# Eight dK stores as GpSimd scatters behind the next Q scaling, in place of five dV stores

## The chip, the cores and the metric

The kernel runs on one core of a Trainium2 chip. A core has five engines with queues of their own: TensorE (PE in the profile; its weight loads are PEld), VectorE (DVE), ScalarE (ACT), GpSimd (POOL) and SyncE (SP). Sixteen DMA engines move data between HBM and the on-chip memory SBUF; matmuls write to PSUM. A transfer that SyncE issues is given to the DMA engines in hardware (queue q1 in the profile); for one that GpSimd issues, software on GpSimd writes what each DMA engine is to do (queue q0). Fetches of program code go over the same 16 engines (q8, q14).

The metric is the time of one execution on the device in microseconds: 669.41 us is the median of 3 runs of the kernel before (668.9 to 669.71). Beside these there is one execution under the profiler, from which all durations below come.

## The reference, cut to what matters

The kernel computes grouped-query attention and its gradients: the output o, and dq, dk and dv for a given `grad_out`.

```python
B, Hq, Hkv, Sq, Sk, D = 32, 32, 4, 4, 2048, 128      # all bfloat16

def _fwd_reference(q, k, v):
    k = jnp.repeat(k, Hq // Hkv, axis=1)
    v = jnp.repeat(v, Hq // Hkv, axis=1)
    scores = jnp.einsum("bhqd,bhkd->bhqk", q, k) * D ** -0.5
    p = _softmax(scores, axis=-1)
    return jnp.einsum("bhqk,bhkd->bhqd", p, v)

def reference(q, k, v, grad_out):
    out, vjp = jax.vjp(_fwd_reference, q, k, v)
    return (out, *vjp(grad_out))
```

K and V are read once and dK and dV written once: 32 batches x 4 heads x 2048 x 128 of two bytes are 67 MB for each of the four, and with q, grad_out, o and dq some 272 MB in all.

## The kernel before, in words

The batch is the outer loop, and one batch is one stage of about 20 us. In HBM, K, V, dK and dV stand as two tensors each (half 0 and half 1, two heads per half), with 128 rows per batch: a row has 4096 bfloat16 (`ROW`, 8192 bytes). Half 0 and half 1 of K carry 128 columns more, q and grad_out (`LONG`, 8448 bytes); half 1 of dV and of dK carry o and dq there. So a batch has four loads (LK and LV, halves 0 and 1) and four stores (SV and SK, halves 0 and 1), each of 128 rows, about 1 MB.

All of them go through 20 row tiles in SBUF (`slots`, `row` in the profile). A slot is filled by a load, read, overwritten by results or the next load, and stored.

The stages of a batch, by the names in the kernel: transposes of q and grad_out (QT), of K and V (KT, VT) on PE and their copies out of PSUM (KTe, VTe and so on, on ACT or DVE); scores (S), row minimum (MX), exponential (EX), reciprocal (RC); on GpSimd the scaling of grad_out by the reciprocal (dop, line 290), a small product (rs, line 302) and the scaling of q (qp, line 293); the transposes of the probabilities (ET) and the output (O, Oe); dP (DP) and dS (DS); their transposes (DT) and dQ (DQ, DQe); dV and dK (DV, DK, line 334) and their evictions to row tiles (DVe, DKe, line 340).

The order of everything is written out by hand: the string `PLAN` has four characters for each unit (name, part, engine or place, buffer), the loop at its end emits them one after another, and each engine runs its own in that order. The units of neighbouring batches are interleaved: the qp of a batch stands behind the last DKe, the DQe and the SK of half 1 of the batch before.

SyncE issues every load and nearly every store in the order of the plan. Each of its DMAs updates one of eight semaphores in turn and waits until the DMA that had it last has landed, so that at most eight are in flight.

Five stores are not SyncE's. For the batches in `SPREAD` (4, 6, 8, 10, 12) the store of half 0 of dV is made by GpSimd right behind the qp of the following batch, as indirect DMAs (scatters) that take the row numbers from a small tile `at` that holds 0, 1, 2, ... Each of the five is made of two pieces, rows 126 and 127 and then rows 0 to 125, that go to output tensors of their own; the host only puts them back in their places. Two more scatters, of 3 and of 13 words, stand before the first and behind the last of them (`turns`); they store nothing that is used.

Of the kernel before, what the change touches and what calls it, by code (L numbers as in the profile page):

```python
# [10 lines left out]
BF16 = mybir.dt.bfloat16  # L11
# [3 lines left out]
P = 128  # L15
NH = 4
ROW = 2 * 16 * P
LONG = ROW + P
# [3 lines left out]

SPREAD = (4, 6, 8, 10, 12)
PIECES = ((126, 2), (0, 126))

# [143 lines left out]
def kernel(  # L169
# [10 lines left out]
    spread,  # L180
    turns,
):
    nc = tc.nc
# [7 lines left out]
    const_pool, sm_pool = pool("const", 1), pool("small", 4)  # L191
# [6 lines left out]
    at = const_pool.tile([P, 1], mybir.dt.int32, name="at")  # L198
    nc.gpsimd.iota(at[:], pattern=[[0, 1]], base=0, channel_multiplier=1)

    def scatter(out, in_):
        nc.gpsimd.indirect_dma_start(out=out, in_=in_, in_offset=None,
                                     out_offset=bass.IndirectOffsetOnAxis(ap=at[0:in_.shape[0], 0:1], axis=0))

    scatter(turns[0], at[0:3, 0:1])
    junk = const_pool.tile([P, D], BF16, name="junk")
# [26 lines left out]
    def emit(u):  # L233
        b, name, i = u.b, u.name, u.part
        t = T[b]
# [14 lines left out]
        elif name == "QTe":  # L250
            t["qdt"] = sm_pool.tile([P, 2 * P], BF16, name="qdt_sb", bufs=3)
            copy16(u.where, t["qdt"][:], t["qtp"])
# [38 lines left out]
        elif name == "qp":  # L291
            t["qp"] = sm_pool.tile([P, D], BF16, name="qp_sb", bufs=2)
            nc.gpsimd.tensor_scalar(out=t["qp"][:], in0=t["q"], scalar1=t["rinv"][:], scalar2=scale, op0=ALU.mult,
                                    op1=ALU.mult)
            if b - 1 in SPREAD:
                for (first, count), piece in zip(PIECES, spread[SPREAD.index(b - 1)]):
                    scatter(piece, T[b - 1]["DV", "out", 0][first:first + count, 0:ROW])
                if b - 1 == SPREAD[-1]:
                    scatter(turns[1], at[0:13, 0:1])
        elif name == "rs":  # L300
# [24 lines left out]
        elif name == "DS":  # L325
            w = slice(2 * QW * i, 2 * QW * i + 2 * QW)
            nc.vector.scalar_tensor_tensor(out=t["ds"][:, w], in0=t["DP", i], scalar=t["dl"][:], in1=t["e"][:, w],  # L327
                                           op0=ALU.subtract, op1=ALU.mult)
        elif name in ("DV", "DK"):
            i, g = divmod(i, 2)  # L330
            acc = t[name, i, g] = bank(u, 2)
            moving, still = ("e", "dop") if name == "DV" else ("ds", "qp")
            for h in (2 * g, 2 * g + 1):
                nc.tensor.matmul(acc[:, QW * (h % 2):QW * (h % 2) + QW], lhsT=t[still][rows[h], :],  # L334
                                 rhs=t[moving][rows[h], QW * i:QW * i + QW], start=True, stop=True,
                                 tile_position=(32 * h, 0))
        elif name in ("DVe", "DKe"):
            i, g = divmod(i, 2)
            copy = nc.scalar.copy if u.where == "A" else nc.vector.tensor_copy
            copy(out=heads_of(t[name[:2], "out", g])[:, :, QW * i:QW * i + QW],  # L340
                 in_=t[name[:2], i, g].rearrange("p (h c) -> p h c", h=2))
        elif name == "SK" and i in LAST:
            g, first, runs, n = LAST[i]
            part = lambda row: (row[:, 0:ROW].rearrange("p (h c) -> p h c", h=2)[:, :, first:first + n] if runs == 2
                                else row[:, first:first + n])
            nc.sync.dma_start(out=part(dk_r[g][b]), in_=part(t["DK", "out", g]))
        elif name in ("SV", "SK"):
            n = LONG if i else ROW
            if not (name == "SV" and i == 0 and b in SPREAD):
                nc.sync.dma_start(out=(dv_r if name == "SV" else dk_r)[i][b], in_=t["D" + name[1], "out", i][:, 0:n])  # L350
# [48 lines left out]
```

## Time and profile before

| | before |
|---|---|
| median of 3 runs | 669.41 us |
| profiled execution, its own time | 671.37 us |
| its span, first to last instruction | 669.2 us |
| granted TensorE clock, mean | 0.984 |
| PE / DVE / ACT / POOL busy | 91% / 86% / 85% / 8% |
| bytes moved by DMA, mean rate | 273.96 MB, 409 GB/s |
| SyncE's queue q1: packets, MB, share of the 16 engines | 37536, 267.40, 96.3% |
| GpSimd's queue q0: packets, MB, share | 1024, 5.24, 2.0% |
| code fetches q8 and q14: packets, MB | 68 and 24, 1.11 and 0.20 |
| scatters on GpSimd | 12, of about 1 us each |

How to read it: the busy time of an engine is a share of the whole span. The slices divide the span into 40 equal parts, and each digit is a busy share in tenths. The DMA row is the mean over the 16 engines. The queues have the packets that were moved: one packet is one row of a transfer, or a 4-byte word that tells of a landing. The chain is the work that ended last, followed back to what released it; a piece of it that is a DMA reaches from its issue to its landing. In the tables of waits the columns are the waiting engine and line, what it waited for, the total in us, how often, and the longest.

### The profile page before, as it was taken

How to read it: one execution, taken by the hardware profiler on the slowest of the kernel's cores; microseconds unless marked ns; L12 is line 12 of the kernel's file. 1: busy time of each engine (PE TensorE's matmuls, PEld its weight loads, DVE VectorE, ACT ScalarE, POOL GpSimd, SP SyncE). 2: the span in 40 equal slices, each digit the busy share in tenths (PEclk: the TensorE clock that was granted, in tenths of full speed). 3: DMA queues.
4: the chain of work that ended last, by engine and by line, in shares of the span. 5: the costliest groups of instructions: out<-in, count | busy, mean ns of one | idle time of the engine just before them, and what ended most of it. 6: DMA issues, size and time to landing. Idle time of an engine off the chain costs nothing.

```text
span 669.2 us, 20668 instructions
## 1 busy us (share of the span) xinstructions
PE 608.9 (91%) x8768; PEld 399.7 (60%) x8768; DVE 572.6 (86%) x736; ACT 569.7 (85%) x802; POOL 50.8 (8%) x115
## 2 busy tenths in 40 slices
PE   5998999999998999899999999998989999898991
PEld 5665666566665666566666666655656556565650
DVE  1988899898998989799899999978989879888991
ACT  4997899898988889799899999978888879878992
POOL 1000000101010010200000000000000000000000
PEclk9999999999999999999999999989999989989996
DMA  9999999999999999999999999999999999999966
GB/s 347 420 423 423 425 411 424 415 419 423 412 423 415 425 416 416 423 407 422 421 424 422 425 425 423 424 423 423 419 408 415 420 421 420 410 417 422 404 276 247
DMA packets 38652, 273.96 MB, mean 409 GB/s; under 512 B 4512, under 2 KB 4512, under 8 KB 6560
## 3 DMA queue, kind: packets, MB, share of 16 engines
q1 hardware_dynamic: 37536, 267.40, 96.3%
q0 software_dynamic: 1024, 5.24, 2.0%
q8 instruction: 68, 1.11, 0.6%
q14 instruction: 24, 0.20, 0.1%
HBM read 136.31 MB, written 136.31 MB: 407 GB/s over the span
## 4 chain that ended last, share of the span: by engine, by line
PE 63%; DMA 17%; ACT 7%; DVE 7%; issue 4%; SPq 0%; DVEq 0%; ACTq 0%
PE psum L260 33%; DMA out_dram<-row 16%; PE psum L334 13%; PE psum L312 9%; PE psum L274 8%; ACT row L340 5%; DVE vt_sb L228 4%; DMA row<-in_k_dram 1%; DVE row L340 1%; DVE ds_sb L327 1%; ACT e_sb L283 1%; PE psum L249 0%; DVE row L320 0%; DVE e_sb L279 0%; ACT vt_sb L226 0%
## 5 line engine op out<-in xcount | busy, mean ns | idle before, releaser
L340 ACT CAST row<-psum 128x1024 bf16<-128x1024 f32 x292 | 291.5, 1021 | 47.6 <-PE psum L334 43.9
L260 PE MATMUL psum<-ident,row 128*128 128x128 f32 x2048 | 287.3, 282 | 12.9 <-DMA row<-in_k_dram 6.8
L340 DVE CAST row<-psum 128x1024 bf16<-128x1024 f32 x220 | 265.0, 1218 | 16.2 <-PE psum L334 7.6
L260 PEld LDWEIGHTS psum<-ident,row 128*128 128x128 f32 x2048 | 223.6, 143 | 78.0 <-issue 24.8
L226 ACT COPY kt_sb<-psum 128x512 f32<-128x512 f32 x190 | 110.3, 600 | 10.4 <-PE psum L260 10.3
L226 ACT COPY vt_sb<-psum 128x512 f32<-128x512 f32 x160 | 92.1, 603 | 27.1 <-PE psum L260 23.2
L327 DVE SCALAR_TENSOR_TENSOR ds_sb<-psum,delta,e_sb 128x1024 bf16<-128x1024 f32 x64 | 82.1, 1283 | 12.2 <-PE psum L274 8.0
L334 PE MATMUL psum<-ds_sb,qp_sb 32*128 32x512 bf16 x512 | 76.9, 383 | 3.4 <-ACT row L340 1.1
L279 DVE TENSOR_SCALAR_CACHE_REDUCE e_sb<-psum 128x2048 bf16<-128x2048 f32 x32 | 73.3, 2291 | 5.8 <-PE psum L274 5.8
L334 PE MATMUL psum<-e_sb,dop_sb 32*128 32x512 bf16 x512 | 69.7, 386 | 8.7 <-DVE row L340 7.6
L228 DVE COPY vt_sb<-psum 128x1024 bf16<-128x1024 bf16 x96 | 60.6, 684 | 8.4 <-PE psum L260 8.1
L283 ACT ACTIVATE e_sb<-psum,m 128x2048 bf16<-128x2048 f32 x32 | 64.0, 2001 | 0.2 <-DVE e_sb L279 0.2
L290 POOL TENSOR_SCALAR dop_sb<-row,rinv 128x128 bf16<-128x128 bf16 x32 | 19.4, 605 | 582.5 <-DVE rinv L287 565.1
L228 DVE COPY kt_sb<-psum 128x1024 bf16<-128x1024 bf16 x66 | 44.9, 682 | 12.4 <-PE psum L260 12.0
L260 PE MATMUL psum<-ident,ds_sb 128*128 128x128 f32 x256 | 41.8, 286 | 9.4 <-DVE vt_sb L228 6.8
L312 PE MATMUL psum<-row,et_sb 128*32 128x128 bf16 x2048 | 41.5, 222 | 6.8 <-issue 6.6
L312 PE MATMUL psum<-row,dt_sb 128*32 128x128 bf16 x2048 | 44.1, 226 | 3.0 <-issue 2.5
L334 PEld LDWEIGHTS <-qp_sb 32*128 32x128 bf16 x512 | 19.4, 91 | 45.8 <-issue 42.2
L312 PEld LDWEIGHTS <-et_sb 128*32 128x32 bf16 x2048 | 31.6, 95 | 23.6 <-issue 12.9
L260 PEld LDWEIGHTS psum<-ident,ds_sb 128*128 128x128 f32 x256 | 26.9, 140 | 27.1 <-DVE vt_sb L228 16.2
L274 PE MATMUL psum<-vt_sb,qdt_sb 128*32 128x512 bf16 x512 | 40.5, 390 | 2.4 <-issue 2.0
L312 PEld LDWEIGHTS <-dt_sb 128*32 128x32 bf16 x2048 | 31.6, 97 | 18.1 <-issue 17.2
(32 smaller groups left out, 320.1 us busy)
## 6 DMA issues: line engine op xcount, KB each, us to landing
out_dram<-row SPq DMA_DIRECT2D x63, 1056.0 KB
row<-in_k_dram SPq DMA_DIRECT2D x62, 1056.0 KB
row<-in_v_dram SPq DMA_DIRECT2D x62, 1024.0 KB
out_dram<-row SPq DMA_DIRECT2D x58, 1024.0 KB
row<-in_v_dram SPq DMA_DIRECT2D x4, 512.0 KB
out_dram<-row SPq DMA_DIRECT2D x3, 512.0 KB
row<-in_k_dram SPq DMA_DIRECT2D x2, 544.0 KB
row<-in_k_dram SPq DMA_DIRECT2D x2, 512.0 KB
```

Of the source, the lines that this page charges most:

```text
L226: nc.scalar.copy(out=out.bitcast(FP32), in_=in_)
L228: nc.vector.tensor_copy(out=out, in_=in_.bitcast(BF16))
L260: nc.tensor.transpose(out=ps[:, P * j:P * j + P], in_=src[:, 4 * half + j, :], identity=ident32[:])
L274: nc.tensor.matmul(out[r, QW * w:QW * w + QW], lhsT=t["qdt"][:, P * side + 32 * h:P * side + 32 * h + 32], rhs=t[x, NH * i + h][:, QW * w: ...
L279: nc.vector.tensor_scalar(out=t["e"][:], in0=t["S"], scalar1=-scale, scalar2=None, op0=ALU.mult, op1=ALU.min, accum_out=t["m"][:])
L283: nc.scalar.activation(out=t["e"][:], in_=t["S"], func=ACT.Exp, bias=t["m"][:], scale=scale, accum_out=t["l"][:])
L290: nc.gpsimd.tensor_scalar(out=t["dop"][:], in0=t["go"], scalar1=t["rinv"][:], scalar2=None, op0=ALU.mult)
L312: nc.tensor.matmul(t[name][r, :], lhsT=left[:, j, r, odd], rhs=right[:, 4 * i + j, :, odd], start=(i == 0 and c == 0), stop=(i == 1 and c ...
L327: nc.vector.scalar_tensor_tensor(out=t["ds"][:, w], in0=t["DP", i], scalar=t["dl"][:], in1=t["e"][:, w], op0=ALU.subtract, op1=ALU.mult)
L334: nc.tensor.matmul(acc[:, QW * (h % 2):QW * (h % 2) + QW], lhsT=t[still][rows[h], :], rhs=t[moving][rows[h], QW * i:QW * i + QW], start=Tr ...
L340: copy(out=heads_of(t[name[:2], "out", g])[:, :, QW * i:QW * i + QW], in_=t[name[:2], i, g].rearrange("p (h c) -> p h c", h=2))
```

## The change

Eight stores of half 1 of dK (batches 5, 7, 10, 13, 15, 18, 21 and 23) leave SyncE and become scatters on GpSimd, behind the qp of the following batch; the five stores of half 0 of dV go back to SyncE. Five of the eight are cut into 120 + 8 rows, three into 85, 3, 34 and 6. The table in front of it names, for each piece, a number from 0 to 15 at which it is to start and its number of rows; a new function `pieces` works out which scatters of words have to stand in between for that, with `shares(n)`, the largest number up to 16 that divides n. That makes 22 scatters of rows and 15 of words, against 10 and 2.

The row of half 1 of dK is 8448 bytes long, that of half 0 of dV 8192. The scatter of 3 words ahead of the first batch is gone. The space for the scatters' descriptors goes from 256 to 1024, and the tile with the transposed q and grad_out (`qdt`) has two buffers in place of three. The plan is the same, and so are all instructions of PE, ACT and DVE and their order. SyncE has 255 DMAs instead of 258.

```diff
-SPREAD = (4, 6, 8, 10, 12)
-PIECES = ((126, 2), (0, 126))
+PAST_ONE = ((5, 120), (15, 8))
+PAST_NINE = ((15, 85), (4, 3), (7, 34), (9, 6))
+SPREAD = {5: PAST_ONE, 7: PAST_NINE, 10: PAST_ONE, 13: PAST_ONE, 15: PAST_NINE, 18: PAST_ONE, 21: PAST_ONE, 23: PAST_NINE}
+
+def shares(n):
+    return max(k for k in range(1, 17) if n % k == 0)
+
+def pieces():
+    at, out = 0, []
+    for b, move in SPREAD.items():
+        row = 0
+        for engine, n in move + ((0, 0),) * (b == max(SPREAD)):
+            turn = (engine - at) % 16
+            for words in (turn,) if turn > 1 else (8, 9) if turn else ():
+                out.append((b, None, words))
+            if n:
+                out.append((b, row, n))
+            row, at = row + n, engine + shares(n) if n else 0
+    return out
...
-    scatter(turns[0], at[0:3, 0:1])
...
-            t["qdt"] = sm_pool.tile([P, 2 * P], BF16, name="qdt_sb", bufs=3)
+            t["qdt"] = sm_pool.tile([P, 2 * P], BF16, name="qdt_sb", bufs=2)
...
-            if b - 1 in SPREAD:
-                for (first, count), piece in zip(PIECES, spread[SPREAD.index(b - 1)]):
-                    scatter(piece, T[b - 1]["DV", "out", 0][first:first + count, 0:ROW])
-                if b - 1 == SPREAD[-1]:
-                    scatter(turns[1], at[0:13, 0:1])
+            for (of, row, n), piece in zip(pieces(), spread):
+                if of == b - 1:
+                    scatter(piece, at[0:n, 0:1] if row is None else T[of]["DK", "out", 1][row:row + n, :])
...
-            if not (name == "SV" and i == 0 and b in SPREAD):
+            if not (name == "SK" and i == 1 and b in SPREAD):
                 nc.sync.dma_start(out=(dv_r if name == "SV" else dk_r)[i][b], in_=t["D" + name[1], "out", i][:, 0:n])
...
-    nc = _bacc.Bacc("TRN2", target_bir_lowering=False, num_devices=1, dynamic_dma_scratch_size=256)
+    nc = _bacc.Bacc("TRN2", target_bir_lowering=False, num_devices=1, dynamic_dma_scratch_size=1024)
```

More of the change, by code (lines that the diff above doesn't have):

```diff
@@ L180 @@
     spread,
-    turns,
 ):
@@ L385 @@
         args.append(nc.dram_tensor(f"out_{i}_dram", shape, dt, kind="ExternalOutput").ap())
-    spread = [[nc.dram_tensor(f"dv0_{b}_{first}_dram", (count, ROW), _mybir.dt.bfloat16, kind="ExternalOutput").ap()
-               for first, count in PIECES] for b in SPREAD]
-    turns = [nc.dram_tensor(f"turn_{n}_dram", (n, 1), _mybir.dt.int32, kind="ExternalOutput").ap() for n in (3, 13)]
+    spread = [nc.dram_tensor(f"piece_{i}_dram", (n, 1 if row is None else LONG),
+                             _mybir.dt.int32 if row is None else _mybir.dt.bfloat16, kind="ExternalOutput").ap()
+              for i, (b, row, n) in enumerate(pieces())]
     with _tile.TileContext(nc) as tc:
-        kernel(tc, *args, spread, turns)
+        kernel(tc, *args, spread)
     r = _run(nc, [arrays], core_ids=[0])
     dk0, dk1, dv0, dv1 = (_np.asarray(r.results[0][f"out_{i}_dram"]) for i in range(len(_OUTS)))
-    dv0 = dv0.copy()
-    for b in SPREAD:
-        for first, count in PIECES:
-            dv0[b, first:first + count] = _np.asarray(r.results[0][f"dv0_{b}_{first}_dram"])
+    dk1 = dk1.copy()
+    for i, (b, row, n) in enumerate(pieces()):
+        if row is not None:
+            dk1[b, row:row + n] = _np.asarray(r.results[0][f"piece_{i}_dram"])
     shape = (32, 32, 4, 128)
```

## The prediction

> **What bounds the kernel now.** I read the page's slices first, then its DMA queues, then the chain that ended last, the stretches of the last 50 us, SyncE's waits, and the GpSimd scatters.
>
> ```profile
> span 669.2 us, 20668 instructions
> ...
> DMA  9999999999999999999999999999999999999966
> ...
> q1 hardware_dynamic: 37536, 267.40, 96.3%
> q0 software_dynamic: 1024, 5.24, 2.0%
> q8 instruction: 68, 1.11, 0.6%
> q14 instruction: 24, 0.20, 0.1%
> ...
> PE 63%; DMA 17%; ACT 7%; DVE 7%; issue 4%; SPq 0%; DVEq 0%; ACTq 0%
> ```
>
> The 16 DMA engines are busy all the way (PE, at 91%, comes behind them), so a microsecond is to be had only where one DMA engine is later than the rest. The chain says that this is so:
>
> ```profile
> 416.08 20.40 DMA out_dram<-row
> 436.55 20.64 DMA out_dram<-row
> ...
> 562.34 21.22 DMA out_dram<-row
> ```
>
> From 416 us on, pieces of the chain are stores that take 20 to 21 us from issue to landing: about 8 MB in front of each at 420 GB/s, because SyncE keeps eight DMAs in flight (the records have each issued once the eighth before it has landed). A DMA has landed only when the last of its 16 shares has. The end:
>
> ```profile
> core 0: us, PE busy (x) PEld busy (x) DVE busy (x) ACT busy (x) POOL busy (x), PEclk, DMA share, GB/s
> ...
> 400.00:420.00 20.00, 19.65 (x317) 12.87 (x315) 18.66 (x25) 18.65 (x27) 1.20 (x3) 1.00 1.01 423
> ...
> 640.00:650.00 10.00, 9.45 (x187) 5.08 (x187) 9.47 (x14) 9.35 (x12) 1.20 (x3) 1.00 0.48 194
> 650.00:660.00 10.00, 4.35 (x86) 2.34 (x83) 4.63 (x5) 5.99 (x8) 0.00 (x0) 0.88 1.01 404
> 660.00:669.00 9.00, 0.00 (x0) 0.00 (x0) 0.00 (x0) 0.00 (x0) 0.00 (x0) 0.50 0.34 128
> ```
>
> The reader is to see the 0.48 and the 0.34: at both places most engines have nothing to do while something is still late.
>
> Which engine is late follows from the trace's packet and landing records. They hold no engine number, but on one engine a packet starts 3 or 4 ns before the one ahead of it ends, and each SyncE DMA leaves the same row packets and one 4-byte packet on every engine, in order. Linking them splits the packets into 16 chains, up to about 640 us. Per chain, with how late it is at the last load (DMA 241) against the earliest:
>
> ```
> chains            scatter rows  fetch packets (time)     lateness at DMA 50 / 120 / 241
> five plain            45        none to 2                0-0.2 / 3.2-9.0 / 0-0.8
> one plain, "15"       45        7 of 8 KB, 2 of 16 KB    1.3 / 9.4 / 2.4
> eight fetching        45        7-9 of 16 KB (8.1 us)    0.6-3.5 / 9.0-11.4 / 4.5-6.2
> second relieved        5        9 of 8 KB (2.8 us)       1.4 / 0.0 / 1.6
> slow                   5        3 of 8 KB                4.8 / 9.1 / 13.5
> ```
>
> A normal row packet of 8192 B has a period of 306 ns, one of 8448 B 316 ns. The slow chain's row packets are stretched by some 30 us in all, and it loses 4.8 us in its first 110 (4.4%). A fetch packet of 16 KB takes 0.99 us, and the row behind it is about 0.36 us longer. The second relieved chain was not slow before it was relieved; afterwards it runs ahead, and its long packets are first packets of a DMA: it waits for SyncE.
>
> At DMA 241 the landing records have the 15th share at 625.5 us and the 16th at 632.9; at the very last store at 663.2 and 667.9. That one slow engine is the bound.
>
> **The change part by part.** *Where rows go.* Rows of a scatter are spread by the program's own function: n rows go to the largest k up to 16 that divides n, from where the last scatter stopped. The row counts above bear this out for 126 (14 engines x 9) and 2: five scatters, 45 rows on 14 chains, 5 on two. Before, numbered as in the program, engines 3 and 4 are spared 35 rows each of the 40 that five SyncE stores would bring, and the others get 5 more. After, against the 64 rows of eight stores: engine 4 -56; 5 and 6 -16; 9 to 14 -21; 7 and 8 +27; 15, 0, 1, 2 and 3 +32. That is one engine spared, eight eased, seven loaded; the trace has one slow, eight fetching and seven plain (the second relieved among them). I take the slow one for 4, the eight for 5, 6 and 9 to 14.
>
> *The sum*, in lateness at the last load against the mean of the eight fetching chains (5.6 us):
> - slow: now 13.5 - 5.6 = +7.9; its relief goes from 35 x 0.306 = 10.7 us to 56 x 0.316 = 17.7; 7.0 us less.
> - eight fetching: +5 rows (1.5 us) become -16 or -21 (-5.1, -6.6): 6.6 to 8.1 us less.
> - plain: +1.5 us becomes +10.1 (+8.5 with 27 rows): 8.6 (7.0) more. Their place now (-4.8 to -5.6) is bounded by an empty ring; by their own load they would be about 11 ahead (8.1 of fetch and 3.0 of stretched rows that they lack): -2.4 to +3.8.
> - chain "15": now -3.2, by its own fetches -5.4: with 8.6 more, +3.2 to +5.4.
> - second relieved, taken as engine 3: from -10.7 to +10.1, 20.8 more. Its own load is 7.5 us of fetch and what follows, against 11.0 for a fetching chain; without the empty ring it would stand at 7.5 - 11.0 - 10.7 - 1.5 = -15.7. After: +5.1.
>
> So the latest goes from +7.9 to about +5.1, and the last load lands 2.8 us sooner (ends: 7.0 if the slow engine alone counted; 0 if the second relieved engine's stalls, 4.7 us here after nine fetches against 2.2 on "15", are worse than I put them). In the 35 us behind the last load the slow engine loses another 4.4%, 1.5 us, which the new latest does not; the last stores also wait for evictions (15 shares landed together at 663.2), so I take half, 0.7. Sum: -3.5 us.
>
> *Scatters instead of stores on GpSimd and SyncE.*
>
> ```profile
> L202 POOL DMA_INDIRECT dv_dram<-row,at x10: 933/972/1011, 120.2 to 280.3; - x10
> ...
> DMA to landing us min/median/max: 6.1/9.1/12.8
> ```
>
> 37 scatters in place of 12, 1.25 us apart: four or five together hold POOL 5 to 6.3 us behind the Q scaling (L293). Next in its queue is the following batch's dop (L290), 18.4 us later: nothing, with 12 us of cover. The dK rows are complete when the Q scaling runs (DKe and DQe stand ahead of it in the order), so no new wait is queued there. The extra 4-byte packets (6 ns of period each, under 20 on each engine per scatter) come to below 1 us on any engine and lie on eased ones as much.
>
> SyncE loses eight dK stores and gets five dV ones back; a load takes the freed slot.
>
> ```profile
> SPq L245 <- DMA out_dram<-row: 90.7, 24, 5.6
> ```
>
> In these eight places the load was issued at the instant that the dK store landed, 2.6 to 5.4 us after its place in the window was free. From the Q scaling to that load there are 19.6 us (b=5), 22.2 (b=7), 24 to 34 (the rest). Four scatters end after 4 x 1.25 + 12.8 = 17.8 us at most; five with 17 rows on an engine, taken in turn with SyncE's packets (17 x 0.63 = 10.7 us, 4.5 to start, issued fourth), after about 20. So the loads are freed no later than before. I book nothing, since the rings are full anyway; if that cover goes, see D.
>
> *The rest.* The first turn scatter (1.0 us, on an idle POOL), the ring space (256 to 1024) and two Q buffers in place of three (the DVE and PE orders are the same, the reader of the older one is a batch back): nothing; a stall per batch would cost up to 32 x 0.3 us, and can't gain.
>
> The profiled execution took 671.37 us (span 669.2 and 2.2 around it), 1.96 over the median. 671.37 - 3.5 = 667.9; against the median, 669.41 - 3.5 = 665.9.
>
> **The rivals.**
> - A, the forecast: 665.9, between 663 and 668.
> - B, larger gain: the plain engines have more slack than I gave them, and only the slow engine's own 7.0 counts: 662.4. For it: six of them stood 3 to 5.6 ahead even while held back.
> - C, no change: the second relieved engine, 20.8 us heavier, ends as late as the slow one did: 669.4 within 1.3 (0.2%, about what a measurement can tell). For it: its stalls; against: they came with an empty ring.
> - D, slower, scatters that land late: with 17 rows of one piece on an engine, a landing of 30 us instead of 20 would be over the room at b=7 by 8 us and at b=15 by 4.5; the earliest engine's share lands 7.6 us after issue against 3.8 on an empty ring, so 3.8 of each is covered: +4.9, 674.3. It decides from a landing of some 26 us on. Against: 12.8 was the longest of ten. The Trainium skill, "DMA: Bandwidth & Descriptors", Rules for kernel authors, speaks against the change here: transfers under 64 KB are mostly overhead and should be made one; its Anatomy section has 2.0 us fixed for each DMA, so that 25 more would be an estimated 50 us if they stood on the path. By the trace they don't: between issue and landing nobody waits, and this page's cost alone would not make a stage longer.
> - E, slower, the wrong neighbour: both relieved chains got 5 rows, so the trace can't say which is 3 and which 4. If the slow one is 3, it goes from -10.7 to +10.1: 669.4 + 20.8 = 690.2. Against: the split of one, eight and seven fits the chains only with 4 slow.
>
> **How the numbers follow.** A 0.62, B 0.10, C 0.12, D 0.06, E 0.10. Faster is A and B, 0.72; same is C, 0.12; slower D and E, 0.16. The range reaches from 662.0 (B, less 0.4 for the spread of the runs) to 671.0 (C and the shorter D) and leaves out E and the longer D.
>
> **What would show it.** Right: q0 with 8.65 MB; the 16th share at the last load and at the last store no more than some 5 us and 3 us behind the 15th, the lag made by engines that got 32 rows; the slow chain with 8 rows in the middle of the field; the 660 us slice shorter. Wrong: one chain 20 us or more behind with 96 scatter rows (E); SyncE's loads waiting long for scatters (D); or an unchanged last lag (C).

## The result, and the profile after

The changed kernel takes 673.93 us (median of 5 runs, 672.09 to 676.9), the kernel before 669.71 us beside it (median of 5, 668.9 to 673.01): a ratio of 1.0055, 95% interval 1.0028 to 1.0081. It is slower, where 665.9 us and a range up to 671.0 were forecast. In run e9 below, the changed kernel once more, the ratio was 1.0024 (0.9993 to 1.0055). The profiled execution took 676.9 us; it is the slowest of the five, as the one of e9 (675.76 us) is of its twelve, so both show the loss at its largest. All ratios here are made from executions within 1.5% of the fastest of their kernel; only for e12 and e13 does that leave out half of them, and their plain medians are given too.

The page of the changed kernel, with the lines that were shown of before (span, slices, queues, chain by engine) and the granted clock:

```profile
span 675.1 us, 20701 instructions
...
PEclk9999999999997999999899999999999899999997
DMA  9999999999999999999999999999999999999968
...
q1 hardware_dynamic: 37104, 264.00, 94.8%
q0 software_dynamic: 3280, 8.66, 3.4%
...
PE 59%; DMA 23%; ACT 7%; DVE 6%; issue 4%; DVEq 0%; SPq 0%; ACTq 0%
...
PE psum L275 30%; DMA out_dram<-row 13%; PE psum L347 13%; PE psum L325 8%; PE psum L289 8%; DMA row<-in_k_dram 6%; ACT row L353 5%; DMA row<-in_v_dram 4%; DVE vt_sb L243 4%; DVE ds_sb L340 1%; ACT e_sb L298 1%; DVE row L353 1%; PE psum L264 0%; DVE row L333 0%; ACT dt_sb L241 0%
```

The bytes moved as foretold (8.66 MB on q0). On the chain the loads of K and V have 6% and 4% of the span, against 1% in the profile of before. That alone is no sign of the change: in another profile of before (e15 below, 669.37 us) they have 6% and 10%. The two chains by line, of before and of e15:

```profile
PE psum L260 33%; DMA out_dram<-row 16%; PE psum L334 13%; PE psum L312 9%; PE psum L274 8%; ACT row L340 5%; DVE vt_sb L228 4%; DMA row<-in_k_dram 1%; DVE row L340 1%; DVE ds_sb L327 1%; ACT e_sb L283 1%; PE psum L249 0%; DVE row L320 0%; DVE e_sb L279 0%; ACT vt_sb L226 0%
```

```profile
PE psum L260 26%; DMA out_dram<-row 18%; PE psum L334 11%; DMA row<-in_v_dram 10%; PE psum L312 6%; PE psum L274 6%; DMA row<-in_k_dram 6%; ACT row L340 5%; DVE vt_sb L228 3%; DVE ds_sb L327 1%; DVE row L340 1%; ACT e_sb L283 1%; DVE row L320 0%; PE psum L249 0%; ACT dt_sb L226 0%
```

The same stretches of the end as before, from the table of stretches (columns as there: length, busy times, granted clock, DMA share, GB/s):

```profile
400.00:420.00 20.00, 19.64 (x286) 13.37 (x287) 18.81 (x26) 18.69 (x29) 4.88 (x7) 1.00 1.02 421
640.00:650.00 10.00, 9.78 (x88) 6.24 (x87) 9.17 (x11) 9.15 (x14) 0.00 (x0) 1.00 0.83 345
650.00:660.00 10.00, 9.13 (x188) 4.94 (x187) 9.47 (x13) 9.34 (x13) 1.20 (x3) 1.00 0.44 181
660.00:675.00 15.00, 4.13 (x84) 2.26 (x81) 4.08 (x5) 5.43 (x7) 0.00 (x0) 0.73 0.83 323
```

The end itself is shorter: the last load landed at 640.3 us and the last store 34 us later, against 632.9 and 35 before. The last store's 16 shares landed within 1.7 us of each other (4.9 before). The time was lost earlier. Worked out from the landing records, this is how much later the load of half 0 of K of a batch landed than in the profiled execution of before (us):

| load for batch | changed (676.9) | changed again, e9 (675.76) | e2 (672.53) | e17 (671.47) | e18 (669.24) |
|---|---|---|---|---|---|
| 8, before any scatter | 2.4 | 1.0 | 1.2 | 1.3 | 0.9 |
| 12 | 1.7 | 1.6 | 1.4 | -0.6 | 1.1 |
| 14 | 4.9 | 4.7 | 5.7 | 1.8 | 2.7 |
| 17 | 7.5 | 8.4 | 8.1 | 2.0 | 4.5 |
| 19 | 10.0 | 12.0 | 8.5 | 2.9 | 4.4 |
| 22 | 11.3 | 12.8 | 9.2 | 1.4 | 4.9 |
| 27 | 12.8 | 12.1 | 8.9 | 1.6 | 2.8 |
| 31 | 8.4 | 8.5 | 3.9 | 0.7 | -1.1 |
| the last store | 6.2 | 5.1 | 1.9 | 0.0 | -1.4 |

The changed kernel falls behind in steps between 240 and 530 us, while scatters run, and gets some of it back when they are over (they end at 523 us). Its two profiled executions give nearly the same curve. Such a curve also moves without the change: in e4 (before with other buffers) the loads were up to 5.3 us later than in this profile of before, and the last store landed 3.0 us sooner.

Now batch 7, the first finely spread store (so the stores of 85, 3, 34 and 6 rows are called, which put 17 rows on each of seven engines). GpSimd's timeline of the changed kernel (start, length, engine, line, operation, idle time before it and what ended it):

```profile
177.61 0.37 POOL L308 TENSOR_SCALAR qp_sb<-row,rinv 128x128 bf16<-128x128 bf16 x1
178.29 0.93 POOL L218 DMA_INDIRECT piece_dram<-at  x1 [0.31 <-issue]
183.62 1.09 POOL L218 DMA_INDIRECT piece_dram<-row,at  x1 [4.39 <-ACT vt_sb L241]
185.01 0.86 POOL L218 DMA_INDIRECT piece_dram<-row,at  x1 [0.30 <-issue]
186.18 1.08 POOL L218 DMA_INDIRECT piece_dram<-row,at  x1 [0.30 <-issue]
187.57 0.87 POOL L218 DMA_INDIRECT piece_dram<-row,at  x1 [0.30 <-issue]
```

The Q scaling runs ahead of the evictions that stand before it in the written order, since it is on another engine; GpSimd then stands idle for 4.4 us ahead of the first scatter of rows. At all eight places rows come 4.9 to 7.0 us behind the word scatter, 0.8 to 1.1 us behind the end of the eviction of dQ (L333), the last write into that row. The profile of before shows the same lag: there GpSimd's Q scaling ran at 178.92 us, and SyncE issued the store of this row at 184.11, as the first of the two in the second line; at all eight places its store came 4.8 us or more behind the Q scaling.

```profile
178.92 0.38 POOL L293 TENSOR_SCALAR qp_sb<-row,rinv 128x128 bf16<-128x128 bf16 x1
184.11 2.08 SPq L350 DMA_DIRECT2D out_dram<-row  x2
```

And the landing, from the group of the scatters and SyncE's table of waits (line, what for: us, times, longest), and SyncE's timeline:

```profile
L218 POOL DMA_INDIRECT piece_dram<-row,at x22: 858/939/1102, 145.5 to 519.9; - x22
...
DMA to landing us min/median/max: 5.5/11.0/20.6
```

```profile
SPq L260 <- DMA piece_dram<-row,at: 14.9, 4, 7.0
```

```profile
197.59 2.19 SPq L260 DMA_DIRECT2D row<-in_v_dram  x1
207.43 0.33 SPq L260 DMA_DIRECT2D row<-in_k_dram  x1
207.87 1.79 SPq L363 DMA_DIRECT2D out_dram<-row  x2
```

The 34-row and 6-row pieces take 18 to 20.6 us to land (16 to 17 for the 85 rows, 11 to 12.7 for 120 rows). So the load that takes the slot goes out at 207.43, 29.5 us behind the end of the Q scaling (22.2 in before), and SyncE, which works in order, issues nothing from 199.8 to 207.4.

Does this lateness of the issue reach the engines that wait for K and V? The landing records say no. This is how much later than in the profile of before, in us, SyncE issued the load that it had held back, how much later that load landed, and how much later the load landed that it had issued just ahead of the wait (changed kernel; e9):

| finely spread store of batch | held-back load issued | held-back load landed | load ahead of it landed |
|---|---|---|---|
| 7 | 5.9; 7.3 | 1.7; 1.6 | 1.7; 1.6 |
| 15 | 8.2; 9.7 | 7.6; 9.4 | 7.5; 9.4 |
| 23 | 7.8; 8.3 | 10.2; 10.3 | 10.2; 10.3 |

A load that was held back landed no later than one that never waited. The loads were late before the wait: the four issued around the scatters of batch 15 and the four around those of batch 23 took 25.6 us on average from issue to landing (25.7 in e9), where the same loads took 19.2 to 19.7 us in four profiles of before and 22.4 in e18 below, whose scatters put 9 rows on an engine. The 16 shares of one of these loads landed over 20.5 us (13.4 in before). So loads that share the engines with 17 scattered rows land later; what that costs is not the same everywhere, as in e17 below the same loads took 22.0 us, the four around batch 23 beside a finely spread store as well.

What PE does around 204 and 320 us, from its timeline, and the stretches from 200 to 210 and 316 to 326 us of the changed kernel and then of before:

```profile
204.34 0.29 PE L325 MATMUL psum<-row,dt_sb 128*32 128x128 bf16 x1 [2.71 <-issue]
...
320.40 1.94 PE L275 MATMUL psum<-ident,row 128*128 128x128 f32 x8 [3.62 <-DMA row<-in_k_dram]
```

```profile
200.00:210.00 10.00, 7.29 (x100) 4.74 (x98) 4.68 (x8) 4.74 (x7) 0.00 (x0) 0.66 1.01 396
316.00:326.00 10.00, 6.38 (x82) 4.78 (x84) 4.60 (x6) 4.52 (x7) 1.20 (x3) 0.66 1.01 411
```

```profile
200.00:210.00 10.00, 8.63 (x184) 5.46 (x182) 7.66 (x12) 7.44 (x10) 1.75 (x2) 1.00 1.02 421
316.00:326.00 10.00, 8.90 (x186) 5.66 (x185) 8.39 (x13) 8.09 (x13) 1.21 (x3) 1.00 1.01 425
```

At 204 us PE stands still for 2.7 us, then its clock is granted at half for 6.8 us, and it does 100 matmuls in the stretch where it did 184 (the stages are shifted by a few us against before). This pause is no wait for a load: the profile names nothing that PE waited for, and the pause ends 1.4 us behind a 16 KB fetch of program code (q8), which comes over the same DMA engines; so do those at 369.9 and 619.5 us. A pause of 1.4 to 1.9 us stands at the same place in two more profiles of before and in e2, e4, e17 and e18, which have no finely spread store there; in the kernels that have one it is under 1.4 (e11) to 5.0 us (e13). The pause at 320 us is a wait for a load of K, but it lies behind a store of 120 + 8 rows (batch 13), and e18, which is faster than before, has it too:

```profile
318.07 1.90 PE L276 MATMUL psum<-ident,row 128*128 128x128 f32 x8 [3.38 <-DMA row<-in_k_dram]
```

Between 20 and 640 us the clock stood at half for 30.7 us (20.5 in e9), against 10.2 in the profile of before, 3.4 and 10.2 in two more of it, and 17.1 in e4. PE's pauses over 1.4 us add up to 20.6 us (17.1 in e9), against 7.0 to 12.6 in those four. The Trainium skill, "TensorE: Matmul & The Clock Gate", Part 1, has the full clock come back only after a busy window of about 3.4 us; the trace agrees, in that each spell at half clock of the changed kernel lasted 3.4 or 6.8 us. That the lower clock follows from the pauses is the order of things in its two profiles (each spell begins 1 to 4 us behind the start of a pause); in before, two of three spells have no pause over 1.4 us ahead of them, and no run here changes one without the other.

### The profile page after: what moved, and what is told of

It is laid out like the page before. It is cut to its first block, busy times and chain, and to the rows that moved or that the text cites. A ratio compares the mean times of both kernels' runs of the same rounds, so it can differ in the third digit from the quotient of the medians.

```text
span 675.1 us, 20701 instructions
## 1 busy us (share of the span) xinstructions
PE 613.7 (91%) x8768; PEld 404.0 (60%) x8768; DVE 573.3 (85%) x736; ACT 570.5 (85%) x802; POOL 74.0 (11%) x140
## 3 DMA queue, kind: packets, MB, share of 16 engines
q0 software_dynamic: 3280, 8.66, 3.4%
## 4 chain that ended last, share of the span: by engine, by line
PE 59%; DMA 23%; ACT 7%; DVE 6%; issue 4%; DVEq 0%; SPq 0%; ACTq 0%
PE psum L275 30%; DMA out_dram<-row 13%; PE psum L347 13%; PE psum L325 8%; PE psum L289 8%; DMA row<-in_k_dram 6%; ACT row L353 5%; DMA row<-in_v_dram 4%; DVE vt_sb L243 4%; DVE ds_sb L340 1%; ACT e_sb L298 1%; DVE row L353 1%; PE psum L264 0%; DVE row L333 0%; ACT dt_sb L241 0%
## 5 line engine op out<-in xcount | busy, mean ns | idle before, releaser
L275 PE MATMUL psum<-ident,row 128*128 128x128 f32 x2048 | 291.2, 285 | 19.6 <-DMA row<-in_k_dram 11.2
L275 PEld LDWEIGHTS psum<-ident,row 128*128 128x128 f32 x2048 | 226.4, 144 | 86.4 <-issue 31.2
L241 ACT COPY kt_sb<-psum 128x512 f32<-128x512 f32 x190 | 110.5, 599 | 13.9 <-PE psum L275 13.8
L340 DVE SCALAR_TENSOR_TENSOR ds_sb<-psum,delta,e_sb 128x1024 bf16<-128x1024 f32 x64 | 82.1, 1283 | 14.7 <-PE psum L289 10.4
L347 PE MATMUL psum<-e_sb,dop_sb 32*128 32x512 bf16 x512 | 71.1, 394 | 7.3 <-DVE row L353 5.5
L243 DVE COPY vt_sb<-psum 128x1024 bf16<-128x1024 bf16 x96 | 60.7, 685 | 11.7 <-PE psum L275 11.4
L289 PE MATMUL psum<-vt_sb,qdt_sb 128*32 128x512 bf16 x512 | 41.9, 397 | 3.2 <-issue 2.1
L241 ACT COPY dt_sb<-psum 128x512 f32<-128x512 f32 x63 | 38.4, 612 | 3.2 <-PE psum L275 3.1
L325 PEld LDWEIGHTS <-et_sb 128*32 128x32 bf16 x2048 | 30.6, 96 | 14.9 <-ACT et_sb L241 10.3
```

The source lines that it names most:

```text
L241: nc.scalar.copy(out=out.bitcast(FP32), in_=in_)
L243: nc.vector.tensor_copy(out=out, in_=in_.bitcast(BF16))
L275: nc.tensor.transpose(out=ps[:, P * j:P * j + P], in_=src[:, 4 * half + j, :], identity=ident32[:])
L289: nc.tensor.matmul(out[r, QW * w:QW * w + QW], lhsT=t["qdt"][:, P * side + 32 * h:P * side + 32 * h + 32], rhs=t[x, NH * i + h][:, QW * w: ...
L325: nc.tensor.matmul(t[name][r, :], lhsT=left[:, j, r, odd], rhs=right[:, 4 * i + j, :, odd], start=(i == 0 and c == 0), stop=(i == 1 and c ...
```

## The experiments

Names: "dV place" is the store of half 0 of dV, "dK place" that of half 1 of dK as in the change, always in batches 5, 7, 10, 13, 15, 18, 21 and 23 unless said. The diffs are against the changed kernel, cut to what matters.

### First: place, split and buffers apart

Run e1 keeps the change's pieces and moves them to the dV place.

```diff
-scatter(piece, ... T[of]["DK", "out", 1][row:row + n, :])
+scatter(piece, ... T[of]["DV", "out", 0][row:row + n, 0:ROW])
```

> The changed kernel with its eight scatters, engine numbers, row counts and word scatters, but storing half 0 of dV in place of half 1 of dK (8192-byte rows). The dV rows are there when the Q scaling ends, and no load takes their slot. Theory L (late landing: GpSimd waits 5 us for the dK rows, the 17-row pieces land 29 us after the Q scaling, and SyncE's load of the slot, with all behind it, waits up to 7 us for them): GpSimd no longer waits and no load waits for a scatter; at or under the kernel before, 664 to 669. Theory H (the seven loaded engines are the late ones now, by the rows they got): the latest engine stays the latest, 672 to 675.

Measured: 674.35 us against 670.0, ratio 1.0086 (1.0051 to 1.0122). This is theory H's time and not theory L's, and no load of SyncE waits for a scatter there. But the landing is not out of it. The tables of waits of DVE and ACT say otherwise:

```profile
DVE row L353 <- DMA piece_dram<-row,at: 7.6, 2, 4.1
```

```profile
ACT row L353 <- DMA piece_dram<-row,at: 4.4, 2, 2.5
```

In the dV place the slot goes on to an eviction instead of a load, and that eviction waits for the same late pieces: 12.0 us in four waits, and PE waits behind DVE (9.1 us, the longest 4.2; before 7.6 and 1.7). So the run leaves both theories standing.

Run e2 keeps the dK place and makes all eight stores 120 + 8 rows; e3 the same in the dV place; e4 is the kernel before with the change's two Q buffers and descriptor space.

```diff
+SPREAD = {b: PAST_ONE for b in (5, 7, 10, 13, 15, 18, 21, 23)}
```

> The changed kernel with all eight dK stores as 120 + 8 rows and none as 85, 3, 34, 6: engine 4 is spared the same 56 rows, seven engines get 8 more and none gets more than that; GpSimd still waits for the dK rows. Theory H: the loaded engines go back by 24 rows of 0.316 us, 7.6 us, and the slow engine keeps its relief: 662 to 667. Theory L: the pieces of 8 and 9 rows land about 12 us after their issue, in time for the load: 665 to 669. A third theory, S (the wait on GpSimd itself, the ring space or the two Q buffers cost the time): as the changed kernel, 672 to 675.

> Both edits: eight dV stores, all as 120 + 8 rows. Theory H: as the second kernel, 662 to 667. Theory L: as the first kernel or a little under, 664 to 668; against the second kernel it shows what the 5 us wait on GpSimd is worth when nothing lands late: nothing by H and L, some 4 us by S.

> The kernel before with two Q buffers in place of three and 1024 in place of 256 for the scatters' descriptors, nothing else. Theories H and L: as before, 669 to 671. Theory S: 672 or more.

Measured: e2 672.15, 1.0052 (1.0023 to 1.0081); e3 668.72, 0.9994 (0.9966 to 1.0022); e4 668.92, 1.0006 (0.9972 to 1.0039). The buffers cost nothing that can be measured, as booked. Without the finely spread stores nothing waits for a scatter in either place, and still neither comes to the 662 to 667 us that the relief of the slow engine promised. Something else in the 120 + 8 form costs too. And the place matters for this form: e2 takes 3.4 us more than e3, about the 4 us that theory S had given, and its 672.15 us is in theory S's range. The buffers of theory S are excluded by e4; the wait on GpSimd is left, until e18 below.

### Second: what scatters cost by themselves

The packets' own durations gave a candidate. Row packets longer than their usual 309 or 319 ns add up, on the average engine, to 10.1 us in before, 13.8 in e3 and 17.7 in e2; in e2 they come in bursts 5 to 8 us behind the issue of a scatter of words. So: no scatters at all (e5), sixteen whole stores as one scatter of 128 rows (e6), the kernel without scatters plus 28 scatters of sixteen words (e7), and the eight dV stores in before's form of 2 + 126 rows (e8).

```diff
+SPREAD = {}                                                  # e5
+SPREAD = {b: ((0, 128),) for b in range(4, 20)}              # e6
+if b in range(4, 32): scatter(words[b - 4], at[0:16, 0:1])   # e7
+SPREAD = {b: ((3, 2), (5, 126)) for b in (5, 7, 10, 13, 15, 18, 21, 23)}   # e8
```

> No scatter at all: all 64 stores of dK and dV of each half go by SyncE, with the ring space and Q buffers of the changed kernel. It takes the five-store spread of the kernel before away, and is the base of the two runs beside it. Theory F (the fee: a scattered store lengthens row packets on all 16 engines; by the packets' times 0.28 us per engine for each of before's five, 0.87 us for each of the eight 120 + 8 stores): the engines are busy 1.4 us less than before's 662.9 us on average, but the slow engine gets its 35 rows back (10.7 us) and the others lose 5 (1.5 us): its lag at the last loads grows from 7 us behind the 15th to some 19, ratio to before 1.010 to 1.018. Theory B (balance alone counts): the same lag, 1.014 to 1.020. The run does not tell them apart; it fixes where the slow engine stands without relief.

> Sixteen dV stores (batches 4 to 19) as one scatter of all 128 rows: 8 rows on each of the 16 engines, so no engine is eased or loaded, and no words are scattered. Against the kernel without scatters. Theory F: the fee is paid sixteen times: row packets together 4.5 us (at 0.28) to 14 us (at 0.87) longer on the average engine, and the time longer by about as much. Theory B: the rows only change their queue; time and packet times within 0.2% and 1.5 us of the kernel without scatters.

> The kernel without scatters, with one scatter of sixteen 4-byte words behind the Q scaling of batches 4 to 31: 28 of them, one word on each engine, which leaves the spread as it is. Theory W (the fee is made by the word scatters: in the eight dK stores of 120 + 8 rows the rows were 0.45 to 1.1 us longer on the average engine in the 3 us behind seven of eight word scatters): 12 to 28 us more in row packets, and the time longer by as much. Else (words cost only their own 9 ns packets, 28 x 2 x 9 ns = 0.5 us an engine): within 0.2% of the kernel without scatters.

> Eight dV stores, in the same batches as the eight 120 + 8 stores tried before, but in before's form: 2 rows on engines 3 and 4 and 126 on the other 14, with no words between them. Engine 4 carries 8 rows in place of 64, as there; engine 3 too. Against before the slow engine is eased by another 21 rows (6.4 us) and the others get 3 more (0.9 us): its lag at the last load goes from 7.9 us over the fetching engines' mean to 0.6, as the 120 + 8 form should have done. Theory F with the fee in the form (0.28 for this one): fee 8 x 0.28 - 5 x 0.28 = 0.8 us; before less 4 to 6 us, ratio 0.991 to 0.995. Theory F with one fee for any scattered store (0.87): 8 x 0.87 - 1.4 = 5.6 us, which takes the gain away: ratio 0.998 to 1.002. Theory B: 0.990 to 0.994.

Measured, with before at 668.0 us: e5 676.22, 1.0106 (1.0059 to 1.0152); e6 676.74, 1.0117 (1.0070 to 1.0165); e7 684.44, 1.0206 (1.0154 to 1.0258); e8 667.69, 0.9971 (0.9936 to 1.0007). Three things follow. The relief itself is real: taking it away costs 1%, and the 16th share of the last load is then 10.1 us behind the 15th. Scatters of whole stores have no fee: sixteen of them change nothing (0.1%), so theory F falls. Scatters of words do: 28 of them cost 8.2 us, 0.29 us each, with row packets 9.5 us longer on the average engine. They move 64 bytes each. The 120 + 8 form needs seventeen of them, 2 + 126 two. Run e8 lies between the ranges given for it, 0.990 to 0.995 and 0.998 to 1.002; it is taken up again in e14. Of the changed kernel's own fifteen scatters of words e7 does not say what they cost: behind the eight word scatters that stand ahead of its stores, the rows were lengthened by 0.01 to 0.12 us only, in both of its profiles, where it was 0.45 to 1.1 us in e2. Nor is the cost the same where the kernels are: e17 below has the first five stores of e2, and the rows behind the word scatters ahead of them were lengthened by 0.01 to 0.42 us there, by 0.04 to 0.87 us in e2. Why the same scatter costs at one time and not at another stays open.

### Third: is one heavy engine late?

In the changed kernel the 16th share of the last load came 6.4 us behind the 15th. Linked packet by packet, the chain that is late seemed to be one of those with 91 to 96 scatter rows and with 8 KB code fetches, which pointed at engines 3 and 15. So the change once more (e9), and with the 17 rows of a finely spread store kept from engine 3 (e10), from 15 (e11), or from both (e12).

```diff
+PAST_NINE = ((7, 34), (9, 6), (15, 68), (3, 4), (7, 16))    # e10
+PAST_NINE = ((7, 34), (9, 7), (0, 68), (4, 3), (7, 16))     # e11
+PAST_NINE = ((7, 34), (9, 7), (0, 51), (3, 4), (7, 32))     # e12
```

> The changed kernel itself, as the base of the three runs beside it and for a second profile of it. Ratio to before 1.003 to 1.008 as recorded. Theory H (heavy engines: one of the seven engines with 91 to 96 scatter rows has the most work and ends last): again one share 5 us or more behind the 15th at the last load, the eased ones together at 0 to 3 us. Theory X (the profile was a chance, being of the slowest of the five executions): the 16th share within 3 us of the 15th.

> In the three finely spread stores the 17 rows of engine 3 go to the others one by one: it carries 51 rows in place of 96, engines 15, 0, 1 and 2 carry 99, 7 and 8 carry 94, engine 4 carries 11. Theory H3 (the late one of the changed kernel is engine 3, the one that before relieved beside the slow one; its chain has eight 8 KB fetch packets, which only engine 3, 4 and 15 had before): the 12.7 us lag of the 16th share at the last load goes down to the next one's 6 us, and 4 to 6 us of time go with it: 0.991 to 0.994 of the changed kernel, 0.997 to 1.000 of before. Theory H15 (the late one is engine 15): no gain, up to 1 us more than the changed kernel. Theory G (all heavy engines cost alike): gain of at most a fifth of what the changed kernel lost, 1 us.

> The same with engine 15 in place of engine 3: 15 carries 51 rows, 0 to 3 carry 99, 7 and 8 carry 94, 4 carries 11. Theory H15: the changed kernel less 4 to 6 us. Theory H3: no gain, up to 1 us more than the changed kernel. Theory G: a gain of at most 1 us.

> Engines 3 and 15 both spared: 54 rows each, 0, 1 and 2 carry 102, 7 and 8 carry 97, the fetching ones 49 to 54, engine 4 carries 14. Theory H3 or H15: whichever of the two it was, 5 to 7 us less than the changed kernel, so 0.994 to 0.998 of before: the best of the four. If the heavy engines without fetches (0, 1, 2) were late too, they now are, with 6 rows more (1.9 us): then it is no better than the changed kernel, 1.004 to 1.010 of before.

Measured, with before at 671.41 us: e9 672.22, 1.0024 (0.9993 to 1.0055); e10 678.99, 1.0114 (1.0059 to 1.0170); e11 680.03, 1.0127 (1.0082 to 1.0171); e12 1.0134 (1.0056 to 1.0212), the median of all six being 685.08. Every theory missed: sparing the suspects made it worse, and in e9 the last gap was 2.2 us, not 6.4. What also grew is the wait of SyncE for scatters. In e10, then e9:

```profile
SPq L260 <- DMA piece_dram<-row,at: 20.8, 6, 7.5
```

```profile
SPq L260 <- DMA piece_dram<-row,at: 14.7, 4, 5.8
```

It is 17.2 us in six waits in e11 and 23.0 in six in e12. These splits end with a piece of 16 or 32 rows over all engines, behind the 17 rows of the heavy ones, and a piece lands up to 23.9 us after its issue in e10. But the wait alone does not make the time: the profile of e10 is of an execution of 673.67 us, 2.1 us shorter than the one of e9, with 6 us more of this wait and the clock at half for only 6.8 us between 20 and 640 us (20.5 in e9).

### Fourth: bursts or totals, and the margin of the slow engine

Run e13 has bursts both ways in the dV place, so that the totals of the engines come closer; e14 repeats e8; e15 and e16 are two more profiles of the kernel before.

```diff
+PAST_TEN = ((5, 22), (0, 4), (9, 102))
+SPREAD = {5: PAST_ONE, 7: PAST_NINE, 10: PAST_TEN, 13: PAST_ONE, 15: PAST_NINE, 18: PAST_TEN, 21: PAST_ONE, 23: PAST_NINE}
```

> The dV version of the changed kernel's split (ratio 1.0086), with a third kind of batch: of the eight stores three are still 17 rows on seven engines, but two (batches 10 and 18) put 17 to 19 rows on engines 9 to 14 and 0 to 2 on the rest, and three are 120 + 8. The totals come closer: 79 to 82 scatter rows on the heavy engines in place of 91 to 96, 65 in place of 43 on engines 9 to 14, 34 on 5 and 6, 6 on engine 4. Theory T (totals: the engine with the most work ends last): 14 rows less on the heavy ones, 4.4 us: between the eight 120 + 8 stores (0.9994) and the version with three (1.0086), so 1.001 to 1.004. Theory P (the burst itself: 17 rows on some engines at once put these 11 to 18 us behind while the others run dry, as the last share is 8 DMAs or 20 us of work from the first; three bursts cost 5.6 us): five bursts cost 9 us, 1.012 to 1.016.

> The eight dV stores of 2 + 126 rows once more, to narrow its interval: 0.9971 [0.9936, 1.0007] in twelve executions. If the executions of before fall in two groups (665 to 669 and 670 to 674 us) because the slow engine is late in the second, this kernel, which eases it by 21 rows more, has few above 669: 0.995 to 0.998. If the groups have another cause, it has as many above 670 as before: 0.999 to 1.001.

> The kernel before, for another profile. At the last load the 16th share was 7.4 us behind the 15th in an execution of 671.4 us, and 1.0 us in one of 667.9 us of the same spread (with other ring space and Q buffers). Theory S (one slow engine late makes the slower executions): over 4 us if this one takes 670 us or more, under 3 us if it takes 668.5 us or less. Theory N (the two have nothing to do with each other): no such order.

> As the look before it: the 16th share over 4 us behind the 15th at the last load if the execution takes 670 us or more, under 3 us if it takes 668.5 us or less; without such an order theory S falls.

Measured, with before at 670.63 us: e13 1.0061 (1.0021 to 1.0101), from 669.84 to 689.14 us, the median of all twelve being 679.68 (1.0135). The first number lies between the two theories, the second in the range of theory P. The closer totals did not help; the spread is the widest of all kernels here. Its waits, from DVE's and ACT's tables:

```profile
DVE row L354 <- DMA piece_dram<-row,at: 23.5, 5, 6.9
```

```profile
ACT row L354 <- DMA piece_dram<-row,at: 15.5, 5, 5.2
```

That is one wait of each for every finely spread store. In its profile (686.09 us) PE's clock was at half for 41.0 us before 640 us, and the 16 shares of the last load landed within 3.6 us of each other: the DMA engines, as even as in no other run, had become the ones that wait.

Run e14 took 664.43 us, 0.9913 (0.9884 to 0.9942): before's form with three more stores is faster than before. The looks at before took 669.37 us, with the 16th share of the last load 2.9 us behind the 15th, and 672.25 us with 5.5 us; beside 1.0 us in 667.95 us (e4) and 7.4 us in 671.37 us (the profile behind the prediction), from which the theory was made. Of the two new ones 672.25 us is as theory S has it; 669.37 us lies between its bounds and tests nothing.

### Fifth: the same rows with more room, and before's form in the dK place

Run e17 keeps the change's rows for each engine and puts the finely spread stores where the load of the slot comes latest, 33 to 34 us behind the Q scaling. Run e18 is the change with before's form.

```diff
+SPREAD = {5: PAST_ONE, 7: PAST_ONE, 10: PAST_ONE, 13: PAST_ONE, 15: PAST_ONE, 20: PAST_NINE, 23: PAST_NINE, 26: PAST_NINE}   # e17
+SPREAD = {b: ((3, 2), (5, 126)) for b in (5, 7, 10, 13, 15, 18, 21, 23)}   # e18
```

> The changed kernel's split with the same rows per engine in all (96 on five engines, 91 on two, 43 to 48 on eight, 8 on engine 4), but the three finely spread stores are those of batches 20, 23 and 26, and 5, 7, 10, 13 and 15 are 120 + 8. In these three the load that takes the slot comes 33 to 34 us behind the Q scaling, in place of 22 to 30 in batches 7 and 15; the last of the finely spread scatters lands 26 to 30 us behind it. Theory L (the late landing costs: SyncE waits 14.9 us for scatters, then PE for the loads behind, then the clock drops): SyncE waits under 4 us for scatters, half-clock time between 20 and 640 us falls from 20 to 31 us to the 10 to 17 of before, and the ratio to before is 0.994 to 1.001. Theory H (the totals of the heavy engines cost, wherever the bursts lie): as the changed kernel, 1.002 to 1.008.

> The eight dK stores of the change, at its place and in its batches, but in before's form: 2 rows on engines 3 and 4 and 126 on the other 14. The same in the dV place took 0.9971 and 0.9913 of before. If only the split costs, this is 0.991 to 0.998 too. If the place costs as well (GpSimd waits 5 to 6 us for the dK rows, and the slot goes to a load 20 to 30 us behind; eight 120 + 8 stores took 1.0052 there against 0.9994 in the dV place), it is 0.997 to 1.003. SyncE's waits for scatters tell how: none expected, with 9 rows on an engine landing some 13 us after their issue.

Measured, with before at 670.54 us: e17 671.35, 1.0026 (0.9991 to 1.0061); e18 668.75, 0.9964 (0.9939 to 0.9988). In e17 half of SyncE's wait for scatters is left,

```profile
SPq L260 <- DMA piece_dram<-row,at: 7.5, 3, 3.8
```

the half clock fell to 17.1 us, and its loads hardly fall behind (the table above). By its time it is theory H's (1.002 to 1.008) and not theory L's (0.994 to 1.001), though its interval reaches into both; against its own before it loses 0.8 us, just as e9 does (672.22 against 671.41). So with half the wait gone and the loads in time again, no gain can be measured: the late landing is not borne out as the cost. Up to batch 15 its stores are those of e2, and yet its loads were 2.0 us late at batch 17, where those of e2 were 8.1. Run e18 has no wait for scatters at all; its scatters land in at most 11.7 us:

```profile
DMA to landing us min/median/max: 5.7/11.0/11.7
```

It differs from the changed kernel in nothing but the split: same place, same batches, same 56 rows off the slow engine, GpSimd waiting for dK as there. It is faster than both kernels. So the split costs the difference: 1.0055 / 0.9964, 0.9%, about 6 us (by e9's 1.0024, 0.6%, 4 us). The wait on GpSimd, which e18 shares, does not make a kernel slower than before by itself. That the place is free is not shown: for 2 + 126 rows the dK place has 0.9964, the dV place 0.9971 and 0.9913; for 120 + 8 it has 1.0052 against 0.9994; for the change's split 1.0055 and 1.0024 against 1.0086.

| kernel | place | split | row and word scatters | waits for scatters, us | ratio to before |
|---|---|---|---|---|---|
| e18 | dK | 2 + 126 | 16, 2 | none | 0.9964 |
| e17 | dK | as changed, later | 22, 13 | 7.5 (loads) | 1.0026 |
| changed; e9 | dK | as changed | 22, 15 | 14.9; 14.7 (loads) | 1.0055; 1.0024 |
| e2 | dK | 120 + 8 | 16, 17 | none | 1.0052 |
| e10, e11, e12 | dK | 17 rows on six or five engines | 25, 11 | 20.8, 17.2, 23.0 (loads) | 1.0114, 1.0127, 1.0134 |
| e8; e14 | dV | 2 + 126 | 16, 2 | none | 0.9971; 0.9913 |
| e3 | dV | 120 + 8 | 16, 17 | none | 0.9994 |
| e1 | dV | as changed | 22, 15 | 12.0 (evictions) | 1.0086 |

## Why the prediction was wrong

The step that failed is the one that gave the scatters no price: "I book nothing" for eight stores in 22 pieces of rows and 15 of words in place of eight stores by SyncE. The runs show 4 to 6 us there: at the same place, in the same batches and with the same 56 rows off the slow engine, the change's split takes 1.0055 and 1.0024 of before, two pieces to a store 0.9964. In the steps of the prediction:

- **Which engine is slow** was right. By the linked packets the slow chain, eased by 56 rows, is in the middle of the field in the profile after. All shares of the last load landed within 12.7 us, so none is 20 us behind; rival E (690.2) falls.
- **The gain of easing it** was right in kind. No run has the change's rows without its pieces, so the -3.5 itself was not measured. In before's form, which eases two engines and loads none by much, 4 to 6 us were expected ahead of e8, and three runs gave 0.3%, 0.9% and 0.36% (1.9, 5.8 and 2.4 us). The step that read "the latest goes from +7.9" rested on one execution in which the slow engine stood 7.4 us behind the next. In others it was 1.0, 2.9 and 5.5, so the gain is smaller in many executions.
- **"The dK rows are complete when the Q scaling runs"** and so no new wait is queued there: this failed. The written order binds each engine, not one engine to another: GpSimd was ahead of ACT and DVE, and the rows went out 4.9 to 7.0 us behind the word scatter at each of the eight places. In e18, which has the same wait, it did not take the gain away; but it makes the landing later.
- **"So the loads are freed no later than before"** failed as a fact. The rows came 5 us later, and the fourth piece took 18 to 20 us from its issue instead of 15, so the load at batch 7 went out 29.5 us behind the Q scaling instead of 22.2, and SyncE waited 14.9 us in all. The price put on it, nothing "since the rings are full anyway", was right as far as the landings show: the held-back loads landed no later than the loads issued ahead of them. Rival D, to which 0.06 was given, put this wait at 674.3; that the median came to 673.93 is luck, since by its mechanism the held-back loads should have landed late by their wait.
- **The second relieved engine at +5.1** was about right as a distance: the 16th share of the last load was 6.4 and 2.2 us behind the 15th in the two profiles. But the last load landed 7.5 us later, not 2.8 us sooner. The sum counts rows on each engine and looks at them once, at the last load. It left out the loads in flight beside the scatters: those took 25.6 us instead of 19.7, and landed up to 12.8 us later than in before while the scatters ran.
- **That 25 more scatters make no stage longer** was too bold. Between the two forms in the dK place, with the same rows off the slow engine (e2 and e18), lie fifteen word scatters, 64 rows on engine 3, and 0.9%, 5.9 us; in the dV place the same two forms lie 0.2% (e8) and 0.8% (e14) apart. Run e7 has 0.29 us for each word scatter, 4.4 us for fifteen. The rule of the Trainium skill that was weighed and set aside ("DMA: Bandwidth & Descriptors", Rules for kernel authors: transfers under 64 KB are mostly overhead and belong together) holds in its direction. By the 2.0 us for each DMA that the Trainium skill has on that page (Anatomy of one DMA), fifteen would be an estimated 30 us; the runs show at most some 0.4 us each.
- **Ring space and Q buffers at nothing** was right (e4, 1.0006).

Shown is that the split makes the change slower, and that the buffers, the wait on GpSimd and the relief do not by themselves. What in the split costs is open. SyncE's wait for late pieces is not borne out: the held-back loads land with the others, e17 with half the wait is no faster than e9, and e10 has a short execution with more of it. The heavier engines (91 to 96 scatter rows; e17 keeps them and its loss), the bursts of 17 rows beside the loads (e13 has five instead of three and is no faster) and the fifteen word scatters (e7) are left, and no run here separates them.

## What to carry to other kernels

To ease one late DMA engine, move rows with the fewest pieces and the fewest rows on any one engine: the same 56 rows off the slow engine gave 0.9964 in two pieces and 1.0055 in four or five. Before a store is given to another engine, add up its way from the latest producer, not from the place in the written order, through the landing of its last piece to the next user of the buffer, and compare that with the next user's time. Count the rows of a burst against the loads in flight beside it, and not only in the total at the end. Read from the landings, and not from the issue, whether a wait of the queue costs anything. And look at the margin of "the last one" in more than one profile before a gain is read from it.

## What was not expected of the hardware

- A scatter of sixteen 4-byte words lengthened the rows on all 16 engines by 0.45 us on average, 5 to 8 us behind its issue, and cost 0.29 us of the time each in e7; in the changed kernel such scatters lengthened them by at most 0.12 us. Sixteen scatters of 128 rows cost nothing (0.1%).
- In the two profiles of the changed kernel all nine pauses of PE of 2.0 to 4.1 us were followed by 3.4 or 6.8 us at half the clock; in before and in e18 one pause of 2.0 us was not.
- Loads that SyncE issued 6 to 10 us later than in before landed no later than the loads that it had issued ahead of them (1.6 to 10.3 us late, both).
- Executions of the kernel before differ in how far the slow DMA engine is behind at the last load: 2.9, 7.4 and 5.5 us in 669.37, 671.37 and 672.25 us, and 1.0 us in 667.95 us with other buffers (e4).
